# A transformer block on one core: stored results of one query block loaded ahead of the attention's end, two weight loads moved, five casts moved to GpSimd

## The chip, the cores and the metric

The kernel runs on one core of one Trainium2 chip. The metric is the device time of one execution in microseconds (us). The engines are TensorE (PE, with PEld for its weight loads), VectorE (DVE), ScalarE (ACT), GpSimd (POOL) and SyncE (SP), which here only issues DMA transfers.

## The reference

One block of a transformer with conditioned layer norms, for 2048 tokens of width 448, all in float32:

```python
mod = (_silu(c) @ w_mod).reshape(c.shape[0], 6, 1, -1)
sa, ca, ga, sb, cb, gb = (mod[:, i] for i in range(6))
h = _layernorm(x) * (1 + ca) + sa
x = x + ga * attention(h, wqkv, wo)          # 16 heads of 28, full softmax, then @ wo
h = _layernorm(x) * (1 + cb) + sb
y = _layernorm(h)
x = x + gb * (gelu(y @ w1 + b1) @ w2 + b2)   # 448 -> 1792 -> 448
```

## The kernel before

Products in full precision are made of three: an operand is split into a high part, rounded to TensorE's faster float32 form (a cast), and a low part, the rest (a subtraction), and high by high, high by low and low by high are summed. So each weight and each activation needs a cast and a subtraction before it is used.

The attention goes through 16 units. A unit is one of 4 groups of four heads and one of 4 blocks of 512 queries (blocks 0 to 3), group by group; so units 12 to 15 are the last group's blocks 0 to 3. A unit has 16 steps, one for each 128 keys: TensorE makes scores (`s`), ScalarE takes their exponentials (`slot_c`, `slot_c0h`, `slot_d` and others), TensorE sums them with the values (`o`). Beside this TensorE computes the scores once more in the other layout (`m`, and `s` in a pair) for the units to come, and VectorE takes their row maxima (`mxp`). Side work hangs on step numbers: `at(step, fn)` puts `fn` on a list, and behind the matmuls of each step the loop runs what is listed for it. Each engine takes its instructions in the order in which this Python code issues them; nothing reorders them. SP's queue is one such order: an issue that waits holds up all behind it.

A unit's output is scaled by its softmax sums (tasks `t_den`, `t_rec`, `t_split`, `t_split2`, some steps into the next unit), split into high and low, and stored: groups 0 to 2 in `dpk` (named `o` in the trace), and unit 14, the last group's block 2, in `down` (named `w`). `project` then multiplies 128 tokens of a block by the output weights `wo` and adds to `acc`. It wants four things of the block: the high rows, the low rows, the mixed rows (the third group's rest, both parts, in four pieces), all loaded by `load_o`, and the last group's own part. For blocks 0 and 1 this happens within the attention; block 2 (`NB - 2`) is projected in the MLP's first iterations, and block 3 later.

The output weights are prepared at steps 178 to 188 (`wo_item`): GpSimd multiplies the raw weights by `ga`, the first product is cast for the high part (`wo_p[0]`, `slot_e` in the trace), and GpSimd subtracts for the low part (`wo_p[1]`).

Behind the attention comes the MLP: for each block, 14 iterations of a first product (`mlp1`, 11 matmuls, gelu on ScalarE, split) and, two iterations later, a second product (`mlp2`, 12 matmuls). W1 and W2 are prepared by `w_prep`, a list of items in order of use: W1's first quarter (items 0 to 3), W2's first quarter (4 to 7), W1's second (8 to 11), and so on. An item's raw tile (one of three, `raw`) is loaded by SP two items ahead, then VectorE casts and subtracts, in W2's case after a multiplication by `gb` into `full`. Ten items are done in the last unit's steps, the others in the MLP's iterations.

The second layer norm of block 0 runs in the last unit too: its tokens are transposed on VectorE in two halves (`turn` and `slot_a2h`), stored to `y_dr`, and loaded again. Two steps of this matter here: `turn` is written and stored at steps 242 and 243, and the tiles `d0h` and `d0i`, which belong to the maxima of pairs in the first units, are free later until W2's third quarter takes them.

The last unit starts at step 240 (`last0`). What the changed lines do before:

```python
    load_o(NB - 2, 2, "c1")     # behind the last step, ahead of mlp1(0, 0)
    load_o(NB - 2, 3, "c0h")
...
    at(last0 + 2, lambda: w_prep.load(2))
```

Of the kernel before, what the change touches and what calls it, by code (L numbers as in the profile page):

```python
# [13 lines left out]
F32 = mybir.dt.float32  # L14
F32R = mybir.dt.float32r
# [7 lines left out]
D = 448  # L23
# [4 lines left out]
NB = S // 512  # L28
NG = H // 4
NKT = S // 128  # L30
# [19 lines left out]
def tile_adaln_block(ctx: ExitStack, tc: tile.TileContext, x, x_t, wqkv, wo, w1, b1, w2, b2, c, w_mod, out):  # L50
    nc = tc.nc
    pe, act, dve, pool, sp = nc.tensor, nc.scalar, nc.vector, nc.gpsimd, nc.sync
# [27 lines left out]
    def nm(t):  # L80
        uid[0] += 1
        return f"{t}_{uid[0]}"

    def sbt(tag, shape, dt=F32, bufs=1):
        return sb.tile(shape, dt, tag=tag, name=nm(tag), bufs=bufs)

    def slot(tag, shape, dt=F32R):
        return sb.tile(shape, dt, tag="slot_" + tag, name=nm("slot_" + tag), bufs=1)
# [24 lines left out]
    def ps_mx():  # L113
        mx_ring.append(mx_ring.pop(0))
        return ps_tile(mx_ring[-1], 1 if mx_ring[-1] == "m1" else 2)
# [7 lines left out]
    def f(t):  # L123
        return t.bitcast(F32)
# [313 lines left out]
    def put_ones(g):  # L438
        sp.dma_start(f(dscr[1][0][g])[DH:128:32, :], ones_d)
# [22 lines left out]
    def mm_acc(p, terms):  # L462
        for i, (a, b) in enumerate(terms):
            pe.matmul(p, a, b, start=(i == 0), stop=(i == len(terms) - 1))  # L464
# [438 lines left out]
    for n, i in (  # L903
# [7 lines left out]
        p, ts = firsts[n]  # L911
# [4 lines left out]
    for b in range(NB):  # L916
# [11 lines left out]
        for n, (tb, kind, g) in enumerate(tasks):  # L928
# [28 lines left out]
            if more:  # L957
                k = n - (6, 4, 4, 4)[b]
# [66 lines left out]
    wo_p = [slot(f"e{part}", [128, NG, D]) for part in range(2)]  # L1025
# [22 lines left out]
    def wo_item(n):  # L1048
        def ld(r):
            if n == 4:  # L1050
                pool.memset(r[:, :D], 0.0)
                for j in range(4):
                    sp.dma_start(r[32 * j : 32 * j + DH, :D], wo[NP + DH * j : NP + DH * j + DH, :])
                return
            p0 = 0
            for r0, r1 in (((128 * n, 128 * n + 128),), MIX_HI, MIX_LO)[max(0, n - 1)]:
                sp.dma_start(r[p0 : p0 + r1 - r0, :D], wo[r0:r1, :])
                p0 += r1 - r0

        def go(r):  # L1060
            full = sbt("full", [128, 512], bufs=3)
            ps = slice(0, 112 if n == 3 else 128)
            pool.tensor_tensor(out=full[ps, :D], in0=r[ps, :D], in1=rows["ga"][ps], op=ALU.mult)

            def rest():
                if n == 3:
                    hi = sbt("hi", [128, 512], F32R, bufs=3)
                    dve.tensor_copy(hi[ps, :D], full[ps, :D])
                    pool.tensor_tensor(out=wo_p[1][ps, 2, :], in0=full[ps, :D], in1=f(hi)[ps, :D], op=ALU.subtract)
                    pool.tensor_copy(wo_p[1][0:32, 2, :], f(hi)[0:32, :D])  # L1070
                    return
                k = min(n, 3)
                dve.tensor_copy(wo_p[0][:, k, :], full[:, :D])
                if n != 2:
                    pool.tensor_tensor(out=wo_p[1][:, k, :], in0=full[:, :D], in1=f(wo_p[0])[:, k, :], op=ALU.subtract)

            at(WO_AT + 2 + 2 * n, rest)

        return ld, go
# [5 lines left out]
    down = [dr.tile([128, 512], F32R, tag=f"w{part}", name=f"w{part}", bufs=1) for part in range(2)]  # L1085
    o_in = {}

    def load_o(qt, n, tag):
        t = slot(tag, [128, 2, 512])
        o_in[(qt, n)] = t  # L1090
        cs = slice(qt * 512, (qt + 1) * 512)
        if n < 2:
            sp.dma_start(f(t), f(dpk[n])[0:256, cs].rearrange("(k p) n -> p k n", p=128))
        elif n == 2:
            for k, pieces in enumerate((zip((0, 1), MIX_HI), zip((1, 0), MIX_LO))):
                p0 = 0
                for part, (r0, r1) in pieces:
                    sp.dma_start(f(t)[p0 : p0 + r1 - r0, k, :], f(dpk[part])[r0:r1, cs])
                    p0 += r1 - r0
        else:  # L1100
            for part in range(2):
                sp.dma_start(f(t)[:, part, :], f(down[part]))

    def wo_terms(qt, own):
        hi, lo, mix = (o_in[(qt, n)] for n in range(3))
        w_hi, w_lo = wo_p
        terms = []
        for k in range(2):
            terms += [(hi[:, k], w_hi[:, k, :]), (hi[:, k], w_lo[:, k, :]), (lo[:, k], w_hi[:, k, :])]
        terms += [(mix[:, 0], w_hi[:, 2, :]), (mix[0:112, 1], w_lo[0:112, 2, :])]  # L1110
        o_hi, o_lo = own
        return terms + [(o_hi, w_hi[:, 3, :]), (o_hi, w_lo[:, 3, :]), (o_lo, w_hi[:, 3, :])]

    def project(qt, t, own):
        p = ps_mx()
        ts = slice(t * 128, (t + 1) * 128)
        mm_acc(p[:, :D], [(x[:, ts], w) for x, w in wo_terms(qt, own)])
        if qt >= NB - 2:
            dve.tensor_tensor(out=acc[qt][:, t, :], in0=p[:, :D], in1=acc[qt][:, t, :], op=ALU.add)
            return  # L1120
        y = sbt("full", [128, 512], bufs=3)[:, :D]
        act.copy(y, p[:, :D])
        pool.tensor_tensor(out=acc[qt][:, t, :], in0=acc[qt][:, t, :], in1=y, op=ALU.add)
# [67 lines left out]
    def ln2_stages(b):  # L1191
# [27 lines left out]
        halves = {}  # L1219

        def turn(t):
            if b:
                if t == 0:
                    turned.append(slot("e1", [128, 14, 4, 32], F32))
                to = turned[0][:, :, t, :]
            else:
                if t == 0:
                    turned.append(None)
                if t % 2 == 0:
                    halves[t // 2] = slot("a2h", [128, 14, 2, 32], F32) if t else sbt("turn", [128, 14, 2, 32])  # L1230
                to = halves[t // 2][:, :, t % 2, :]
            dve.transpose(to, ys[t][:, :D].rearrange("p (c j) -> p c j", j=32))

# [25 lines left out]
        for t in range(4):  # L1259
            own = 20 if 0 < b < NB - 1 else 0  # L1260
            at_stage = (
                (t, 4 + t, 6 + t, 10 + t // 2, 10 + t),
                (t, 4 + t, min(6 + t, 8), 9, 30 + t),
                (t // 2, 2 + t // 2, 4 + t // 2, 6 + t // 2, own + 10 + t),
            )[min(b, 2)]
            for i, fn in zip(at_stage, (lambda t=t: stat(0, t), lambda t=t: mid(t), lambda t=t: stat(1, t), lambda t=t: fin(t), lambda t=t: addb(t))):
                plan.setdefault(i, []).append(fn)
            plan.setdefault(11 + t // 2 if not b else 10 if b < 2 else 7 + t // 2, []).append(lambda t=t: turn(t))
# [79 lines left out]
    NU = NG * NB  # L1348
    sched = {}

    def at(step, fn):
        sched.setdefault(step, []).append(fn)

    wo_prep = Prep([wo_item(n) for n in range(5)])
    for i in range(2 * NC):
        h, k = divmod(i, NC)
# [21 lines left out]
    for qt in range(NB - 2):  # L1378
        for n, tag in enumerate(("a2h", "a3h", "b1h")):
            at(NKT * (NU - NB + qt + 1) - 3, lambda qt=qt, n=n, tag=tag: load_o(qt, n, tag))  # L1380
    for n, tag in enumerate(("a3h", "b1h")):
        at(NKT * (NU - 1), lambda n=n, tag=tag: load_o(NB - 2, n, tag))
    for i in range(5):
        at(1 + i, lambda: put_spare(1))
    for g in (1, 2):
        at(6 + g, lambda g=g: put_ones(g))
    at(WO_AT + 11, b2_load)
    at(WO_AT + 24, b2_mul)
    last0 = NKT * (NU - 1)
# [12 lines left out]
    items += [w1_item(3, k, ("c1", "c1h")) for k in range(NC)]  # L1402
    items += [w2_item(ft, ("e0",)) for ft in range(12, NFT)]
    w_prep = Prep(items)
    at(last0 + 2, lambda: w_prep.load(2))
    for k in range(10):
        at(last0 + 5 + k + (k >= 4), w_prep.step)

# [46 lines left out]
    for u in range(NU):  # L1455
        g, qt = divmod(u, NB)
# [71 lines left out]
    def mlp1(b, i, mid=None):  # L1528
        q, ii = divmod(i, 4)
        w_hi, w_lo = w1t[q]  # L1530
        fs = slice(ii * 128, (ii + 1) * 128)
        p = ps_mx()
        ts = terms448(*yT[b], lambda k: w_hi(k)[:, fs], lambda k: w_lo(k)[:, fs])
        mm_acc(p, [(w, y) for y, w in ts])
        if mid:
            mid()
        gf = sbt("full", [128, 512], bufs=3)
        if (b, i) == (0, 0):
            act.activation(gf[:, 0:1], zero_col, AF.Gelu_apprx_tanh)
        act.activation(gf, p, AF.Gelu_apprx_tanh, bias=b1_col[:, i : i + 1])  # L1540
        ghi = sbt("hi", [128, 512], F32R, bufs=3)
        glo = sbt("lo", [128, 512], F32R, bufs=3)
        (dve.tensor_copy if b else act.copy)(ghi, gf)  # L1543
        dve.tensor_tensor(out=glo, in0=gf, in1=f(ghi), op=ALU.subtract)  # L1544
        gs[(b, i)] = (ghi, glo)

    load_o(NB - 2, 2, "c1")
    load_o(NB - 2, 3, "c0h")
    mlp1(0, 0)
    av(*pend)  # L1550
    end_unit(pend[0], pend[3])
    tail = {}
    assert len(sched) == 8
    for t in range(4):
        tail[1 + t] = [lambda t=t: project(NB - 2, t, [o_in[(NB - 2, 3)][:, part] for part in range(2)])]
    tail[1].append(lambda: load_o(NB - 1, 1, "c1h"))
    tail[4] += [lambda: load_o(NB - 1, 0, "c1"), lambda: load_o(NB - 1, 2, "b1h")]
    for n, k in zip((0, 0, 4, 5, 6, 7, 8, 8), sorted(sched)):
# [91 lines left out]
```

## Time and profile before

| | |
|---|---|
| median of 3 runs | 1086.80 us (1086.71 to 1086.81) |
| the profiled execution's own time | 1086.78 us |
| its span | 1085.0 us |
| mean granted TensorE clock | 0.997 of full speed |
| busy share of the span | PE 99%, PEld 60%, DVE 74%, ACT 64%, POOL 24% |

The profile is one execution of the program, its times counted from the start of the span. A row of the timeline has the start, the time that the rows merged in it take, the engine, the line of the code (`L464` is the helper in which most products are issued, so there the names tell more), the operation, what it writes and reads, and in square brackets how long the engine had been idle before it, and what ended that. `SPq` rows are DMA issues on SyncE's queue. The page's row of the granted clock, in tenths for 40 equal slices of the span, drops from 9 in one slice alone:

```profile
PE   8999999999999999999999999999989999999998
PEclk9999999999999999999999999999989999999999
```

The place of that 8 is the slice from 787 to 814 us (30th of 40 slices of 27.1 us), just behind the last unit.

### The profile page before, as it was taken

The numbers are of one execution on the slowest core, as the hardware profiler recorded it, in microseconds if no ns is written. First come the engines' busy times: TensorE is split into PE (matmuls) and PEld (weight loads), VectorE is DVE, ScalarE is ACT, GpSimd is POOL, SyncE is SP. The second block draws the span as 40 slices with busy tenths as digits, with TensorE's granted clock in tenths as the row PEclk, the third lists the DMA queues.
The fourth block names the chain that finished last, engine by engine and source line by source line (L and its number), as shares of the span: only waits on it lengthen the run. The fifth ranks groups of instructions, "written<-read, shape, count | busy, mean of one in ns | idle before, by whom it ended". The sixth has DMA issues, their size and how long they took to land. (4 is left out here: it accounts for less than half of the span.)

```text
span 1085.0 us, 20661 instructions
## 1 busy us (share of the span) xinstructions
PE 1070.8 (99%) x8175; PEld 652.1 (60%) x8175; DVE 797.9 (74%) x1361; ACT 693.8 (64%) x874; POOL 264.2 (24%) x240
## 2 busy tenths in 40 slices
PE   8999999999999999999999999999989999999998
PEld 6766764444444444444444444554478888888887
DVE  6977878999999989888888887675555565464322
ACT  4567768888888888888888888778833321211111
POOL 1586620011001101034512410126414032061000
PEclk9999999999999999999999999999989999999999
DMA  9444370111231111343434330113543301002000
GB/s 312 174 172 146 122 233 21 61 53 52 63 103 59 50 48 28 96 122 83 126 94 120 112 105 31 58 31 94 151 130 96 105 35 43 31 34 73 34 1 34
DMA packets 70335, 95.99 MB, mean 88 GB/s; under 512 B 22331, under 2 KB 34894, under 8 KB 70226
## 3 DMA queue, kind: packets, MB, share of 16 engines
q1 hardware_dynamic: 69754, 93.93, 28.2%
q8 instruction: 64, 1.05, 0.4%
q10 hardware_dynamic: 148, 0.46, 0.1%
q0 software_dynamic: 336, 0.28, 0.1%
q14 instruction: 33, 0.27, 0.1%
HBM read 64.73 MB, written 31.57 MB: 89 GB/s over the span
## 5 line engine op out<-in xcount | busy, mean ns | idle before, releaser
L550 DVE TENSOR_REDUCE mxp<-m 128x1 f32<-128x512 f32 x554 | 358.9, 686 | 69.9 <-PE m L545 58.4
L1492 PE MATMUL s<-slot_b,slot_a 28*128 28x512 f32 (+1 forms) x3072 | 356.6, 425 | 0.1
L1492 PEld LDWEIGHTS s<-slot_b,slot_a 28*128 28x128 f32 (+1 forms) x3072 | 210.5, 183 | 181.3 <-ACT slot_c L1505 99.9
L545 PE MATMUL m<-kh,qh 28*128 28x512 f32 x593 | 217.2, 473 | 0.0
L1505 ACT ACTIVATE slot_c<-s 128x1024 f32<-128x1024 f32 x170 | 174.7, 1027 | 51.1 <-PE s L1492 50.3
L1447 PE MATMUL o<-slot_c,v 128*32 128x512 f32 x680 | 178.9, 605 | 0.0
L1540 ACT ACTIVATE full<-m,b_col 128x512 f32<-128x512 f32 x56 | 38.5, 688 | 196.0 <-PE m L464 187.5
L759 DVE TENSOR_REDUCE mxp<-s 128x2 f32<-128x1024 f32 x117 | 143.4, 1226 | 6.0 <-PE s L545 0.8
L1447 PE MATMUL o<-slot_c1h,v 128*32 128x512 f32 x512 | 134.7, 605 | 0.0
L1447 PE MATMUL o<-slot_c0h,v 128*32 128x512 f32 x508 | 133.6, 605 | 0.0
L1505 ACT ACTIVATE slot_c1h<-s 128x1024 f32<-128x1024 f32 x128 | 130.8, 1022 | 0.0
L1505 ACT ACTIVATE slot_c0h<-s 128x1024 f32<-128x1024 f32 x127 | 130.5, 1028 | 0.0
L1505 ACT ACTIVATE slot_d<-s 128x1024 f32<-128x1024 f32 x86 | 88.3, 1026 | 26.1 <-PE s L1492 25.5
L1543 DVE CAST hi<-full 128x512 fp32r<-128x512 f32 x42 | 19.0, 453 | 102.8 <-ACT full L1540 102.7
L545 PEld LDWEIGHTS m<-kh,qh 28*128 28x128 f32 x593 | 86.2, 181 | 12.7 <-DVE mxp L550 10.9
L1447 PE MATMUL o<-slot_d,v 128*32 128x512 f32 x344 | 90.5, 605 | 0.4 <-ACT osb L1411 0.4
L1148 POOL TENSOR_TENSOR osb<-osb,osb 128x512 f32<-128x512 f32 x16 | 20.5, 1281 | 283.1 <-DMA osb<-drec 262.3
L1544 DVE TENSOR_TENSOR lo<-full,hi 128x512 fp32r<-128x512 f32 x56 | 46.1, 824 | 27.6 <-ACT hi L1543 22.2
L464 PE MATMUL m<-y,slot_a 128*128 128x512 f32 x160 | 60.3, 393 | 0.1
L545 PE MATMUL s<-kh,qh 28*128 28x512 f32 x234 | 52.0, 439 | 0.0
L1447 PEld LDWEIGHTS o<-slot_c,v 128*32 128x32 f32 x680 | 24.5, 108 | 38.4 <-issue 36.6
L723 DVE CUSTOM_DVE_ANT_0 slot_d0i<-m,slot_d0i 128x512 f32<-128x512 f32 x51 | 35.3, 692 | 14.6 <-PE m L545 12.1
(370 smaller groups left out, 1845.4 us busy)
## 6 DMA issues: line engine op xcount, KB each, us to landing
slot_b<-d SPq DMA_DIRECT2D x32, 256.0 KB
slot_a<-d SPq DMA_DIRECT2D x32, 256.0 KB
d<-lo SPq DMA_DIRECT2D x28, 256.0 KB
d<-hi SPq DMA_DIRECT2D x16, 256.0 KB
osb<-drec SPq DMA_DIRECT2D x15, 256.0 KB
out_dram<-xn SPq DMA_DIRECT2D x16, 224.0 KB
raw<-in_B_w_dram SPq DMA_DIRECT2D x14, 224.0 KB
qh<-d SPq DMA_DIRECT2D x12, 256.0 KB
```

Source lines behind the costliest of these rows:

```text
L464: pe.matmul(p, a, b, start=(i == 0), stop=(i == len(terms) - 1))
L545: pe.matmul(m, qh_sb[(g, qt)][js, i * 128 : (i + 1) * 128], k[js, :], start=True, stop=True)
L550: dve.tensor_reduce(out=mxp[(g, qt)][:, i, j, cch : cch + 1], in_=m, op=ALU.max, axis=AX.X)
L723: dve.tensor_tensor_reduce(out=r, in0=p, in1=r, scale=1.0, scalar=-3.0e38, op0=ALU.add, op1=ALU.max, accum_out=mxp[(g, qt)][:, i, j, cch + ...
L759: dve.tensor_reduce(out=mxp[(g, qt)][:, i, j : j + 2, cch], in_=t, op=ALU.max, axis=AX.X)
L1148: pool.tensor_tensor(out=st["on"], in0=o_sb, in1=st["rb"], op=ALU.mult)
L1447: pe.matmul(o[32 * j : 32 * j + 32, :], v_sb[kt // 4][:, kt % 4, 4 * g + j, :], p[j // 2][:, j % 2, :], start=(kt == 0), stop=(kt == NKT - 1),
L1492: pe.matmul(s2[:, jj, :], ks[rows_, kp, kc], qs[rows_, qp, :], start=(term == 0), stop=(term == 2))
L1505: act.activation(pt[hf], s2, AF.Exp, scale=SCALE)
L1540: act.activation(gf, p, AF.Gelu_apprx_tanh, bias=b1_col[:, i : i + 1])
L1543: (dve.tensor_copy if b else act.copy)(ghi, gf)
L1544: dve.tensor_tensor(out=glo, in0=gf, in1=f(ghi), op=ALU.subtract)
```

## The change

It has three parts. The loads of block 2's mixed rows and of its own part move from behind the last step to steps 248 and 253, into other tiles: the mixed rows into `turn`, which gets the size of two rows of 512, and the own part into `d0h` and `d0i`. W1's first two raw loads move from step 242 to step 234. And the five casts of `wo_item` move from VectorE to GpSimd.

```diff
             def rest():
                 if n == 3:
                     hi = sbt("hi", [128, 512], F32R, bufs=3)
-                    dve.tensor_copy(hi[ps, :D], full[ps, :D])
+                    pool.tensor_copy(hi[ps, :D], full[ps, :D])
...
                 k = min(n, 3)
-                dve.tensor_copy(wo_p[0][:, k, :], full[:, :D])
+                pool.tensor_copy(wo_p[0][:, k, :], full[:, :D])
...
+    def load_own(qt):
+        o_in[(qt, 3)] = [slot(tag, [128, 1, 512])[:, 0, :] for tag in ("d0h", "d0i")]
+        for part in range(2):
+            sp.dma_start(f(o_in[(qt, 3)][part]), f(down[part]))
+
     def load_o(qt, n, tag):
-        t = slot(tag, [128, 2, 512])
+        t = slot(tag, [128, 2, 512]) if tag != "turn" else sbt(tag, [128, 2, 512], F32R)
...
-                    halves[t // 2] = slot("a2h", [128, 14, 2, 32], F32) if t else sbt("turn", [128, 14, 2, 32])
+                    halves[t // 2] = slot("a2h", [128, 14, 2, 32], F32) if t else sbt("turn", [128, 2, 512]).rearrange(
+                        "p a n -> p (a n)"
+                    )[:, : 2 * D].rearrange("p (c t j) -> p c t j", t=2, j=32)
...
+    at(NKT * (NU - 1) + 8, lambda: load_o(NB - 2, 2, "turn"))
+    at(NKT * (NU - 1) + 13, lambda: load_own(NB - 2))
...
-    at(last0 + 2, lambda: w_prep.load(2))
+    at(last0 - 6, lambda: w_prep.load(2))
...
-    load_o(NB - 2, 2, "c1")
-    load_o(NB - 2, 3, "c0h")
...
-        tail[1 + t] = [lambda t=t: project(NB - 2, t, [o_in[(NB - 2, 3)][:, part] for part in range(2)])]
+        tail[1 + t] = [lambda t=t: project(NB - 2, t, o_in[(NB - 2, 3)])]
```

SP's queue before, from the last load of W1's second quarter (two halves) through block 2's mixed rows (`slot_c`, four pieces out of the stored `o`) and its own part (`slot_c0h`, out of the stored `w`) to the next W2 load:

```order
L1311 DMA raw_10922<-in_B_w_dram 64x512
L1312 DMA raw_10922<-in_B_w_dram 64x512
L1098 DMA slot_c_2554_10925<-o_2011 80x512
L1098 DMA slot_c_2554_10925<-o_2012 48x512
L1098 DMA slot_c_2554_10925<-o_2012 32x512
L1098 DMA slot_c_2554_10925<-o_2011 80x512
L1102 DMA slot_c0h_10930<-w_2013 128x512
L1102 DMA slot_c0h_10930<-w_2014 128x512
L1330 DMA raw_10971<-in_B_w_dram 128x448
```

SP's queue now, from the first load of W2's first quarter to the last of W1's second: the mixed rows go into `turn`, the own part into `slot_d0h` and `slot_d0i`, behind the stores `w` of its two parts.

```order
L1334 DMA raw_10683<-in_B_w_dram 128x448
L1103 DMA turn_10707<-o_2011 80x512
L1103 DMA turn_10707<-o_2012 48x512
L1103 DMA turn_10707<-o_2012 32x512
L1103 DMA turn_10707<-o_2011 80x512
L1334 DMA raw_10714<-in_B_w_dram 128x448
L1334 DMA raw_10777<-in_B_w_dram 128x448
L1334 DMA raw_10808<-in_B_w_dram 128x448
L1167 DMA w_2013<-hi_10810 128x512
L1167 DMA w_2014<-lo_10811 128x512
L1313 DMA raw_10844<-in_B_w_dram 128x512
L1091 DMA slot_d0h_10868<-w_2013 128x512
```

The four mixed-row loads moved up past seven weight loads (eight issues) and the two stores, and the own part past three weight loads (four issues): the second own load, then the weight loads of 128x512, follow the last row shown.

GpSimd's order before, from the second multiplication of the raw output weights (`full`) to the first cast of the unit's output (`osb` into `hi`):

```order
L1063 TENSOR_TENSOR full_8396<-raw_8190,row_b2g_8221 128x448
L1075 TENSOR_TENSOR slot_e_488_2010<-full_8330,slot_e_487_2009 128x448
L1063 TENSOR_TENSOR full_8466<-raw_8332,row_b2g_8221 128x448
L1051 MEMSET raw_8468 128x448
L1075 TENSOR_TENSOR slot_e_488_2010<-full_8396,slot_e_487_2009 128x448
L1063 TENSOR_TENSOR full_8537<-raw_8398,row_b2g_8221 112x448
L1063 TENSOR_TENSOR full_8598<-raw_8468,row_b2g_8221 128x448
L1148 TENSOR_TENSOR osb_8404<-osb_8258,osb_8404 128x512
L1069 TENSOR_TENSOR slot_e_488_2010<-full_8537,hi_8601 112x448
L1070 CAST slot_e_488_2010<-hi_8601 32x448
L1158 CAST hi_8639<-osb_8404 128x512
```

GpSimd's order now, from the same multiplication to the cast of the fourth piece:

```order
L1063 TENSOR_TENSOR full_8396<-raw_8190,row_b2g_8221 128x448
L1073 CAST slot_e_487_2009<-full_8330 128x448
L1075 TENSOR_TENSOR slot_e_488_2010<-full_8330,slot_e_487_2009 128x448
L1063 TENSOR_TENSOR full_8466<-raw_8332,row_b2g_8221 128x448
L1051 MEMSET raw_8468 128x448
L1073 CAST slot_e_487_2009<-full_8396 128x448
L1075 TENSOR_TENSOR slot_e_488_2010<-full_8396,slot_e_487_2009 128x448
L1063 TENSOR_TENSOR full_8537<-raw_8398,row_b2g_8221 112x448
L1073 CAST slot_e_487_2009<-full_8466 128x448
L1063 TENSOR_TENSOR full_8598<-raw_8468,row_b2g_8221 128x448
L1150 TENSOR_TENSOR osb_8404<-osb_8258,osb_8404 128x512
L1068 CAST hi_8601<-full_8537 112x448
```

Each cast moved from VectorE's order into GpSimd's, ahead of the subtraction that uses it; a fifth follows the rows shown, and nothing else on either engine changed places.

More of the change, by code (lines that the diff above doesn't have):

```diff
@@ L1093, in load_o @@
             sp.dma_start(f(t), f(dpk[n])[0:256, cs].rearrange("(k p) n -> p k n", p=128))
-        elif n == 2:
+        else:
             for k, pieces in enumerate((zip((0, 1), MIX_HI), zip((1, 0), MIX_LO))):
@@ L1099, in load_o @@
                     p0 += r1 - r0
-        else:
-            for part in range(2):
-                sp.dma_start(f(t)[:, part, :], f(down[part]))
     def wo_terms(qt, own):
```

## The prediction, made before the changed kernel was run

> **What bounds the kernel now.** I read the page's busy shares first, then who TensorE waited for, then the stretch of its longest wait by windows, then that stretch instruction by instruction.
>
> ```profile
> PE 1070.8 (99%) x8175; PEld 652.1 (60%) x8175; DVE 797.9 (74%) x1361; ACT 693.8 (64%) x874; POOL 264.2 (24%) x240
> PE m L464 <- DMA slot_c<-o: 5.7, 2, 4.3
> 778.00:785.60 7.60, 7.54 (x36) 4.83 (x34) 7.29 (x12) 3.87 (x6) 2.81 (x3) 1.00 0.46 145
> 790.00:795.50 5.50, 4.03 (x10) 3.05 (x11) 1.49 (x3) 0.00 (x0) 0.71 (x1) 0.50 0.91 289
> ```
>
> TensorE carries the kernel. Behind the attention, from 778 us to the end, its matmuls waited in one place alone: twice for `slot_c<-o`, together 5.7 us. Those are the stored attention results of block 2, wanted by its first projection. The two windows (columns: length, busy time of PE, PEld, DVE, ACT and POOL, granted clock, DMA share, GB/s) lie ahead of the longer wait and behind it: full clock, then 5.5 us at a granted clock of 0.50. So the wait costs more than its own length. Behind it TensorE waits for nothing more, so whatever is saved here reaches the end.
>
> **Term 1: the wait for block 2's results.**
>
> ```profile
> 785.33 0.36 PE L464 MATMUL m<-slot_e,slot_b1h 128*128 128x448 f32 x1
> 789.96 0.71 PE L464 MATMUL m<-slot_e,slot_c 128*128 128x448 f32 x1 [4.27 <-DMA slot_c<-o]
> 792.14 0.71 PE L464 MATMUL m<-slot_e,slot_c 112*128 112x448 f32 x1 [1.47 <-DMA slot_c<-o]
> ...
> 795.48 0.46 PE L464 MATMUL m<-y,slot_b 128*128 128x512 f32 x1
> ...
> 798.17 0.36 PE L464 MATMUL m<-slot_e,slot_b1h 128*128 128x448 f32 x1
> ...
> 799.39 0.37 PE L1584 MATMUL s<-slot_v,hi 128*128 128x448 f32 x1
> ...
> 801.82 0.39 PE L464 MATMUL m<-y,slot_b 128*128 128x512 f32 x1
> ...
> 802.73 0.39 PE L464 MATMUL m<-y,slot_b 128*128 128x512 f32 x1
> ```
>
> From the last matmul ahead of the wait (785.33) to the first one back near full speed (795.48) pass 10.15 us. In them start six matmuls of a projection and four of an MLP's first product. The next projection does the same six in 799.39 - 798.17 = 1.22 us, the next first product the same four in 802.73 - 801.82 = 0.91 us. So 10.15 - 2.13 = 8.0 us are lost, 5.7 to the wait and 2.3 to the slow clock behind it. With all operands there in time the change gets the 8.0 us back. Are they there? Without the wait TensorE wants the mixed rows at 785.5, the own part (high) at 785.9 and (low) at 786.4.
>
> ```profile
> 759.90 5.93 DMA osb<-drec
> 765.86 0.47 SPq L1312 DMA_DIRECT2D raw<-in_B_w_dram  x1
> 767.48 0.33 SPq L1330 DMA_DIRECT2D raw<-in_B_w_dram  x1
> 773.94 1.95 SPq L1330 DMA_DIRECT2D raw<-in_B_w_dram  x2
> 776.04 0.33 SPq L1165 DMA_DIRECT2D w<-hi  x1
> 777.42 0.33 SPq L1165 DMA_DIRECT2D w<-lo  x1
> 778.86 4.55 SPq L1309 DMA_DIRECT2D raw<-in_B_w_dram  x3
> ...
> 786.52 1.93 SPq L1098 DMA_DIRECT2D slot_c<-o  x4
> 788.56 0.83 SPq L1102 DMA_DIRECT2D slot_c0h<-w  x2
> ```
>
> *Mixed rows, four loads.* Before, they are issued at 786.52, behind every weight load of the last steps. Now they stand ahead of the second W2 load (767.48). Their tile was last read by the stores of the first transposed half, long landed by then. They read results stored units earlier. Their issues take 1.93 us, so even one after another by 773.9, where SP next has something to do, they are 11 us ahead of need: no wait is left here.
>
> *Own part, two loads.* They must follow the stores `w<-hi` (776.04) and `w<-lo` (777.42) and now stand behind the weight load of 778.86. Neither a store's landing nor this load is timed in the trace. The bounds:
>
> ```profile
> 752.37 1.91 DMA y_dr<-turn
> 783.08 2.65 DMA raw<-in_B_w_dram
> ```
>
> A store of the same queue took 1.91 us, a 256 KB load 2.65 us in quiet traffic, 5.93 us (`osb<-drec`) at worst. Low store landed at 777.42 + 1.9 = 779.3; low part issued by 779.9 (one issue is 0.3 to 0.4 us), landed at 782.6 with 2.65 us, at 785.8 with 5.93. All of it is ahead of 786.4. If the store also took 5.93 us: 783.4 + 0.4 + 5.9 = 789.7, a wait of 3.3 us. I take the quiet price, because the windows show 145 GB/s there, half of the 289 of the crowded one; the 3.3 us stay for the range.
>
> *What is queued behind.* Behind the own loads on SP wait the raw loads of W1's second quarter. Each needs a raw tile that VectorE gives back, so that three issues of 0.33 us spread over 4.55 us (778.86 to 783.41); SP's wait for the store until 779.3 and two issues lie inside the first gap, so nothing is pushed. At 786.5 SP is now rid of six issues (2.8 us), which is to the good of the loads after it. The two tiles of the own part were last used many steps earlier, and the W2 quarter that takes them next comes after the last projection.
>
> **What would be late next.** TensorE would come 8 us earlier to everything behind 786 us.
>
> ```profile
> 777.80 1.03 DVE L1340 TENSOR_TENSOR full<-raw,row_gb 128x448 f32<-128x448 f32 x1
> 780.97 1.28 ACT L1539 ACT_TABLE_LOAD   x1 [2.37 <-DVE slot_a L1343]
> 786.27 0.68 ACT L1540 ACTIVATE full<-m,b_col 128x512 f32<-128x512 f32 x1
> 786.40 0.69 DVE L1544 TENSOR_TENSOR lo<-full,hi 128x512 fp32r<-128x512 f32 x1
> 794.01 0.63 DVE L1119 TENSOR_TENSOR acc<-m,acc 128x448 f32<-128x448 f32 x1 [4.82 <-PE m L464]
> 808.98 0.39 PE L464 MATMUL m<-y,slot_v 128*128 128x512 f32 x1
> ```
>
> By the matmul rows a first product takes 2.5 us, a projection 2.2, a second product 2.4. So the next first product starts at 786.6, the second projection at 789.1, the first second product at 791.3, the one after at 793.7. Their needs: the bank of the gelu at 786.27, free at 787.0 (2.1 us to spare); the low part made at 786.40, there at 787.1 (4.2 us); the bank of the first projection, added by VectorE, which idles 4.82 us ahead of 794.01 and so does it at 789.2 (3.9 us). The matmul of 808.98, first on W1's second quarter, would start at 801.0; the last piece of that quarter is prepared right behind the add, now about 790.4. The smallest margin is 2.1 us. Term 1 stays 8.0 us.
>
> **Term 2: five casts from VectorE to GpSimd.**
>
> ```profile
> L1073 DVE CAST slot_e<-full x4: 331/383/385, 594.3 to 612.6; 128x448 fp32r<-128x448 f32 x4
> L1158 POOL CAST hi<-osb x13: 604/610/1008, 218.9 to 775.0; 128x512 fp32r<-128x512 f32 x13
> 607.63 1.00 DVE L1068 CAST hi<-full 112x448 fp32r<-112x448 f32 x1
> 607.09 1.29 POOL L1148 TENSOR_TENSOR osb<-osb,osb 128x512 f32<-128x512 f32 x1
> 608.71 1.16 POOL L1069 TENSOR_TENSOR slot_e<-full,hi 112x448 fp32r<-112x448 f32 x1 [0.33 <-DVE mxp L542]
> 608.80 0.69 DVE L550 TENSOR_REDUCE mxp<-m 128x1 f32<-128x512 f32 x1
> 610.68 1.03 ACT L1505 ACTIVATE slot_c<-s 128x1024 f32<-128x1024 f32 x1 [0.35 <-PE s L1492]
> 613.59 1.02 ACT L1505 ACTIVATE slot_d<-s 128x1024 f32<-128x1024 f32 x1 [0.81 <-PE s L1492]
> 618.02 1.02 ACT L1505 ACTIVATE slot_c<-s 128x1024 f32<-128x1024 f32 x1 [0.37 <-PE s L1492]
> ```
>
> Four casts took 0.33 to 0.39 us; I count no loss for them. The fifth began while GpSimd multiplied (607.09 to 608.38) and took 1.00 us; the maxima behind it, and TensorE which waits for them, came late: the next exponential of the same half waited 0.81 us for TensorE, and the step took 613.59 - 610.68 = 2.91 us, against (618.02 - 613.59) / 2 = 2.2 in the two behind it. That is 0.7 us that go with the cast. Between nothing (another wait takes its place) and 0.7 I take 0.7: the steps behind give nothing back. On GpSimd five casts come in, 0.6 us each by its casts of a 128x512 tile (median 610 ns), 3 us in all on an engine 24% busy, which no longer waits for VectorE there; nothing wants the output weights before the projections units later. The cost is nothing.
>
> The Trainium skill ("SBUF — State Buffer", section "SBUF: two separate sides") has a rule that speaks against this: VectorE and GpSimd share a pair of ports under an exclusive lock, held for the whole instruction, so that each added GpSimd cast may stop a VectorE instruction that needs the pair. What that would do here is the second rival below; with it the sum would be 8.7 - 3 = 5.7 us saved.
>
> **Term 3: W1's first two loads eight steps sooner.**
>
> ```profile
> 749.29 0.95 SPq L1309 DMA_DIRECT2D raw<-in_B_w_dram  x2
> 755.20 0.35 DVE L1321 CAST slot_b<-raw 128x512 fp32r<-128x512 f32 x1
> ```
>
> They move ahead of the last unit's maxima and the loads of block 2's first rows. Two issues, 0.95 us: that much could be won or lost on SP. But VectorE takes the first tile at 755.20 without a wait, and the stores behind them on SP go at 752.37, when VectorE has made their data. The third load, which VectorE does wait for, stays where it was. Zero.
>
> **Sum.** 8.0 + 0.7 = 8.7 us. The profiled execution took 1086.78 us around its span of 1085.0 us and stands on the median (1086.80). So 1086.8 - 8.7 = 1078.1 us, a span near 1076.3.
>
> **Rivals.**
> *A shorter wait stays* (0.13): the own part is late. Priced above: up to 3.3 us of wait, 1081.4 us; if the clock also falls as it did behind the 4.27 us, up to 2.3 more, 1083.7. The Trainium skill ("TensorE: Matmul & The Clock Gate", section "What's actually happening") puts the fall behind an idle window of some 3.4 us; by it a shorter wait can cost only itself, and 1081.4 would stand. The trace shows no wait between 1.5 and 4.3 us that could tell.
> *The added casts hold VectorE up* (0.04): VectorE's fifth cast took 1.00 us beside GpSimd in place of 0.38, so the two do get in each other's way. Were each of five casts of 0.6 us to stop a maximum for its whole length, 3.0 us would be lost: 1081.1 us. Against it: the maximum of 608.80 took its 0.69 us beside GpSimd's 1.16 us, and VectorE does little but maxima there. So far the trace bears the lock out for casts only.
> *The wait only changes its name* (0.05): an eviction or a weight becomes the bound as TensorE comes early. Against it stand the margins of 2.1 us and more; it would have to take 6.5 of the 8.7 us to end within 0.2%, at 1084.6 or above.
> *Slower* (0.03): the four mixed-row issues push the W2 load behind them. SP issues only when an earlier transfer has landed: the issue at 765.86 came the moment `osb<-drec` had (759.90 + 5.93). So that load could go at 773.9 in place of 767.48 and land by 779.8 in place of VectorE's 777.80; the gelu's table load follows VectorE's work on that tile (780.97), and TensorE waits once this is over 2.1 us late. It decides from 2.1 + 8.7 = 10.8 us of delay on, which no transfer of this trace comes near: with 14 us, 1090.0.
> *More is saved* (0.03): freed VectorE time speeds up other steps; 1077 or a little below.
>
> **Numbers.** The forecast has 0.72, its own range 1077.4 to 1079.2 (with no gain from the casts and a wait of some tenths). The range for 8 in 10 reaches below into the last rival and above through the first two: 1076.8 to 1082. A measurement tells about 0.2%, 2.2 us: faster (below 1084.6) has 0.72 + 0.13 + 0.04 + 0.03 = 0.92, same 0.05, slower 0.03.
>
> **What would show it.** Right: TensorE's first projection runs through, the granted clock stays at 1.0 from 785 to 800, VectorE no longer idles 4.8 us, the loads `turn<-o` go out near 767 to 774 and the own loads near 779 to 780; the step at 610 us takes 2.3. Wrong: a wait of TensorE for `slot_d0h` or `slot_d0i`, or for `hi`, `lo` or a weight between 786 and 802.

## The result, and the profile after

| | before | after |
|---|---|---|
| median | 1086.80 us (1086.71 to 1088.67, 4 runs) | 1078.61 us (1077.36 to 1079.04, 4 runs) |
| the profiled execution | 1086.78 us, span 1085.0 | 1077.36 us, span 1075.6 |
| predicted | | 1078.1 us (1076.8 to 1082.0) |

The ratio is 0.9919, with a 95% interval of 0.9901 to 0.9936: 8.2 us faster by the medians. The profiled execution of after is the fastest of its four; its difference to before, 9.4 us, is what the traces below add up to.

The page of after: the busy times and the granted clock in 40 slices.

```profile
PE 1067.0 (99%) x8175; PEld 650.1 (60%) x8175; DVE 796.1 (74%) x1356; ACT 693.6 (64%) x874; POOL 266.7 (25%) x245
PEclk9999999999999999999999999999999999999999
```

The 8 in the clock's 30th slice is gone. TensorE's waits from 700 us to the end, in us, times and the longest, now hold a single row, from the attention; the 5.7 us for `slot_c<-o` have no successor:

```profile
PE o L1453 <- ACT osb L1417: 0.4, 1, 0.4
```

The windows around the block's end (length, busy time of PE, PEld, DVE, ACT and POOL, granted clock, DMA share, GB/s), and TensorE's timeline there, from the last matmul that both kernels share to the fifth of the next first product:

```profile
784.00:788.00 4.00, 4.00 (x20) 3.45 (x19) 3.93 (x9) 2.45 (x4) 0.73 (x2) 1.00 0.68 189
788.00:792.00 4.00, 4.00 (x22) 3.69 (x21) 3.33 (x8) 1.77 (x3) 0.71 (x1) 1.00 0.74 243
```

```profile
783.97 0.36 PE L464 MATMUL m<-slot_e,slot_b1h 128*128 128x448 f32 x1
784.17 0.58 PE L464 MATMUL m<-slot_e,turn 128*128 128x448 f32 x2
784.59 0.57 PE L464 MATMUL m<-slot_e,slot_d0h 128*128 128x448 f32 x2
785.00 0.36 PE L464 MATMUL m<-slot_e,slot_d0i 128*128 128x448 f32 x1
...
786.13 0.39 PE L464 MATMUL m<-y,slot_b 128*128 128x512 f32 x1
```

From `slot_b1h` to the fifth matmul of the first product pass 786.13 - 783.97 = 2.16 us, where before 10.15 us passed: 8.0 us saved, at full clock throughout. At `slot_b1h` this run was already 785.33 - 783.97 = 1.36 us ahead: 0.5 us were there at 580 us, ahead of the first instruction that the change moves (0.2 of them since 16 us, behind loads of the start), 0.6 us came in the steps of the casts (below), and 0.2 us in small pieces behind them. 1.4 + 8.0 = 9.4.

SP's queue in after, with the loads in their new place:

```profile
765.97 3.64 SPq L1103 DMA_DIRECT2D turn<-o  x4
769.71 4.78 SPq L1334 DMA_DIRECT2D raw<-in_B_w_dram  x3
774.63 0.34 SPq L1167 DMA_DIRECT2D w<-hi  x1
776.02 0.33 SPq L1167 DMA_DIRECT2D w<-lo  x1
777.46 0.33 SPq L1313 DMA_DIRECT2D raw<-in_B_w_dram  x1
777.88 0.38 SPq L1091 DMA_DIRECT2D slot_d0h<-w  x1
778.36 0.38 SPq L1091 DMA_DIRECT2D slot_d0i<-w  x1
```

The own part goes out 6.7 and 6.6 us before TensorE takes it at 784.59 and 785.00. The four mixed-row issues take 3.64 us instead of 1.93: by SP's row of waits 1.6 us of it are three waits for earlier loads (`xn<-y_dr`, 1.0 us the longest), and one of the issues itself took 1.28 us, where the four of before took 0.41 to 0.53 each.

### The profile page after: what moved, and what is told of

It reads as the page before. It is cut to its first block, busy times and chain, and to the rows that moved or that the text cites. A ratio compares the mean times of both kernels' runs of the same rounds, so it can differ in the third digit from the quotient of the medians.

```text
span 1075.6 us, 20660 instructions
## 1 busy us (share of the span) xinstructions
PE 1067.0 (99%) x8175; PEld 650.1 (60%) x8175; DVE 796.1 (74%) x1356; ACT 693.6 (64%) x874; POOL 266.7 (25%) x245
## 3 DMA queue, kind: packets, MB, share of 16 engines
q8 instruction: 64, 1.05, 0.4%
## 4 chain that ended last, share of the span: by engine, by line
PE 97%; DVE 1%; DMA 1%; ACT 1%; issue 0%; SPq 0%; ACTq 0%; DVEq 0%
PE s L1498 24%; PE o L1453 24%; PE m L464 17%; PE pa L464 9%; PE m L545 6%; PE s L1588 3%; PE s L1590 3%; PE s L1589 3%; PE s L545 2%; PE ma L545 2%; PE t L1590 1%; PE t L1588 1%; PE t L1589 1%; DMA slot_c<-in_w_mod_dram 1%; PE o L342 0%
```

## The experiments

Three questions were open: which part carries the 8 us, why the clock falls behind a wait, and what the casts are worth. Each group of kernels below is compared with before on the same chip: 1087.05 us there for the three parts alone and the doubled casts, 1087.12 for the late loads, 16 extra matmuls and the one moved cast, 1087.11 for the rest.

### Each part alone

**The loads alone**, on before:

```diff
+    at(NKT * (NU - 1) + 8, lambda: load_o(NB - 2, 2, "turn"))
+    at(NKT * (NU - 1) + 13, lambda: load_own(NB - 2))
...
-    load_o(NB - 2, 2, "c1")
-    load_o(NB - 2, 3, "c0h")
```

> The kernel before with the block-2 loads moved alone (mixed rows into turn at step 248, own part into d0h and d0i at step 253); casts and W1's first loads stay. Theory (the loads carry the gain, 8.0 us of it: 5.7 us of wait and 2.3 us of slow clock): 8.0 us faster than before, 1078.8 us, TensorE without a wait in the first projection, granted clock 1.0 there. Rival (the earlier W1 loads are needed to keep SP's queue and the W2 loads in time): a wait of TensorE or a W2 load that lands late remains, 1080 to 1083 us.

1078.23 us (1077.97 to 1078.92), ratio 0.9919 (0.9904 to 0.9934). TensorE waits no more than in after, and the clock holds:

```profile
788.00:792.00 4.00, 4.00 (x22) 3.65 (x21) 3.37 (x7) 2.21 (x4) 0.71 (x1) 1.00 0.72 236
```

The moved loads carry all of the gain that can be measured, and they need neither of the other parts.

**The casts alone**, on before:

```diff
-                    dve.tensor_copy(hi[ps, :D], full[ps, :D])
+                    pool.tensor_copy(hi[ps, :D], full[ps, :D])
...
-                dve.tensor_copy(wo_p[0][:, k, :], full[:, :D])
+                pool.tensor_copy(wo_p[0][:, k, :], full[:, :D])
```

> The kernel before with the five casts moved to GpSimd alone. Theory: 0.6 us faster than before, 1086.2 us; in the trace the step whose exponential started at 610.68 takes 2.3 us in place of 2.91, and the wait for block 2's results stays at 5.7 us. Rival (shared ports: GpSimd's casts hold VectorE's maxima up): up to 3 us slower, 1089.8 us, with maxima longer than 0.69 and 1.23 us beside the casts.

1086.21 us, ratio 0.9993 (0.9984 to 1.0003). The long step at 610 us is 2.30 us long, as expected; the 0.8 us between the medians is less than the interval resolves.

**W1's loads alone**, on before:

```diff
-    at(last0 + 2, lambda: w_prep.load(2))
+    at(last0 - 6, lambda: w_prep.load(2))
```

> The kernel before with W1's first two loads at step 234 alone. Theory: no change, 1086.8 us; VectorE takes the two tiles at the same distance from the end of the last step as before. Rival (they free SP and the transfers around 750 us): the third and fourth W1 loads land sooner and up to 0.9 us is gained, 1085.9 us.

1086.70 us, ratio 0.9997 (0.9988 to 1.0006): no change. VectorE's waits for the third and fourth load, in before first and in this kernel second (timeline; in brackets the idle time and what ended it):

```profile
766.30 0.43 DVE L1321 CAST slot_b<-raw 128x512 fp32r<-128x512 f32 x1 [8.89 <-DMA raw<-in_B_w_dram]
771.45 1.46 DVE L1321 CAST slot_b<-raw 128x512 fp32r<-128x512 f32 x1 [3.99 <-DMA raw<-in_B_w_dram]
```

```profile
765.23 0.43 DVE L1321 CAST slot_b<-raw 128x512 fp32r<-128x512 f32 x1 [8.62 <-DMA raw<-in_B_w_dram]
770.38 0.51 DVE L1321 CAST slot_b<-raw 128x512 fp32r<-128x512 f32 x1 [3.99 <-DMA raw<-in_B_w_dram]
```

The first two loads were not late, and the two that were are issued where they always were.

### Each of the two loads left late

**The own part behind the last step**, all else as in after:

```diff
-    at(NKT * (NU - 1) + 13, lambda: load_own(NB - 2))
...
+    load_own(NB - 2)
     mlp1(0, 0)
```

> The changed kernel with the loads of the own part left behind the last step (into d0h and d0i as now), the mixed rows at step 248. SP then issues them behind the last weight load of W1's second quarter, in the changed kernel's time at about 785.1 and 785.5; with 2.65 us they land near 788. TensorE wants them at 784.6 and 785.0. Theory: a wait of about 3 us and nothing else, 1081.7 us; if the clock falls as it did behind the wait of 4.27 us, up to 2.3 us more, 1084.0 us. Rival (the loads were ready in time from there too, so that only the mixed rows mattered): 1078.6 us.

1083.91 us (1082.47 to 1084.20, 7 runs), ratio 0.9968 (0.9957 to 0.9979): 5.3 us of the gain gone. SP's issue and TensorE's wait, and the window:

```profile
785.05 0.58 SPq L1091 DMA_DIRECT2D slot_d0h<-w  x1
...
788.13 1.12 PE L464 MATMUL m<-slot_e,slot_d0h 128*128 128x448 f32 x2 [3.41 <-DMA slot_d0h<-w]
789.49 0.74 PE L464 MATMUL m<-slot_e,slot_d0i 128*128 128x448 f32 x1 [0.24 <-DMA slot_d0i<-w]
```

```profile
788.00:792.00 4.00, 3.63 (x8) 2.58 (x9) 1.73 (x3) 0.29 (x1) 0.57 (x1) 0.50 0.72 263
```

A wait of 3.41 us took the clock down as the 4.27 us of before had. From the start of the last `slot_b1h` matmul ahead of the wait to the start of the next projection this trace takes 794.27 - 783.94 = 10.33 us, and after takes 787.71 - 783.97 = 3.74. So 6.6 us are lost here in the traces: 3.65 to the two waits and 2.9 to the slow clock.

**The mixed rows behind the last step**, all else as in after:

```diff
-    at(NKT * (NU - 1) + 8, lambda: load_o(NB - 2, 2, "turn"))
...
+    load_o(NB - 2, 2, "turn")
     mlp1(0, 0)
```

> The changed kernel with the loads of the mixed rows left behind the last step (into turn as now), the own part at step 253. SP issues the four loads at about 785.1 to 787.0; landing takes up to 4 us as before, so the second mixed product starts near 790.5 in place of 784.4. Theory: a wait of some 6 us and the slow clock behind it (2.3 us), so nearly all of the gain is lost: 1085.5 to 1086.9 us. Rival (it was the own part that held the projection): 1078.6 to 1080 us.

1085.86 us (10 runs), ratio 0.9989 (0.9980 to 0.9999): nearly all of the gain gone.

```profile
788.37 0.71 PE L464 MATMUL m<-slot_e,turn 128*128 128x448 f32 x1 [4.29 <-DMA turn<-o]
789.51 0.71 PE L464 MATMUL m<-slot_e,turn 112*128 112x448 f32 x1 [0.42 <-DMA turn<-o]
```

Here too the granted clock is 0.50 from 788 to 792 us. So the loads must both move. With either of the two left late, less than half of the gain is there: the projection needs both, and TensorE waits for whichever comes last.

### Why the clock falls

Two explanations stood against each other: TensorE standing still, or the crowded DMA queues of that stretch (289 GB/s before). In before, extra matmuls whose result is overwritten fill a part of the wait (16 of them, the cut shown), or the whole (32):

```diff
+        if (qt, t) == (NB - 2, 0):
+            for _ in range(16):
+                pe.matmul(p[:, :D], o_in[(qt, 0)][:, 0, ts], wo_p[0][:, 0, :], start=True, stop=True)
```

**16 extra matmuls.**

> The kernel before, its loads where they were, with 16 additional matmuls of 448 columns (0.2 us each, 3.2 us) ahead of block 2's first projection, written to the bank that the projection then starts afresh. They fill part of the wait. Theory (2.3 of the 8.0 us came from the clock, which falls when TensorE stands still for 4.3 us): the transfer ends when it did, the wait ahead of the first mixed product shrinks to about 1.0 us, the clock stays at 1.0 and the time falls by about 2 us to 1084.5 us, though TensorE does more work. Rival (the slow matmuls behind the wait come from the transfers' traffic, 289 GB/s, and not from standing still): they stay slow, 1086.8 us.

1086.69 us (10 runs), ratio 0.9996 (0.9986 to 1.0005): not faster, so the expectation missed.

```profile
783.43 3.40 PE L1119 MATMUL m<-slot_e,slot_a3h 128*128 128x448 f32 x16
...
788.68 0.44 PE L464 MATMUL m<-slot_e,slot_c 128*128 128x448 f32 x1 [0.63 <-DMA slot_c<-o]
790.89 0.44 PE L464 MATMUL m<-slot_e,slot_c 112*128 112x448 f32 x1 [1.77 <-DMA slot_c<-o]
```

```profile
792.00:796.00 4.00, 4.00 (x12) 3.19 (x12) 2.63 (x5) 0.56 (x1) 0.00 (x0) 0.57 0.78 270
```

The waits shrank by 3.3 us, as much as the filler takes. But two short waits, 0.63 and 1.77 us, with one matmul between them, brought the slow clock too, and with some delay: the matmuls at 788.68 and 790.89 still ran in 0.44 us, and then it fell, to 0.57 from 792 to 796. That is the profiled execution. Seven of the ten have its mean granted clock of 0.998 and a median of 1087.32 us; three have 1.000 and a median of 1086.15. So the fall may be missing in some executions, of which no trace was kept, but even those are not near the 1084.5 us expected.

**32 extra matmuls.**

> The kernel before with 32 additional matmuls (6.5 us) ahead of block 2's first projection in place of the 16 of the run before, so that TensorE is busy until the transfers land (second mixed product at 790.9 there). Theory (the clock falls because TensorE stands still, also in pieces: 0.63 and 1.77 us with one matmul between were enough): no wait, granted clock 1.0 through 796 us, and though TensorE does 6.5 us more of work, the time falls by the 2.3 us of the clock, to about 1084.7 us. Rival (the clock falls with the transfers' traffic): the matmuls behind 791 us stay slow, 1086.7 us or more.

1084.69 us (10 runs), ratio 0.9979 (0.9969 to 0.9989): 6.5 us of useless work added, and 2.4 us saved.

```profile
783.67 6.65 PE L1119 MATMUL m<-slot_e,slot_a3h 128*128 128x448 f32 x32
...
791.38 0.57 PE L464 MATMUL m<-slot_e,slot_c 128*128 128x448 f32 x2
```

```profile
792.00:796.00 4.00, 4.00 (x20) 3.36 (x19) 2.77 (x5) 1.36 (x3) 0.00 (x0) 1.00 0.83 282
```

No wait for the loads is left and the clock stays at 1.00, beside 282 GB/s. Standing still is the cause, not the traffic. From the start of the first projection, with its filler, to the start of the second this trace takes 794.93 - 783.67 = 11.26 us, before's 797.16 - 784.32 = 12.84: 1.6 of the 2.4 us are shown at this place, the rest lies within the interval (1.2 to 3.4 us).

**The old loads kept beside the new ones**, into two tiles that nothing reads, in after:

```diff
+    o2, o3 = o_in[(NB - 2, 2)], o_in[(NB - 2, 3)]
+    load_o(NB - 2, 2, "c1")
+    idle = slot("c0h", [128, 2, 512])
+    for part in range(2):
+        sp.dma_start(f(idle)[:, part, :], f(down[part]))
+    o_in[(NB - 2, 2)], o_in[(NB - 2, 3)] = o2, o3
     mlp1(0, 0)
```

> The changed kernel with the old loads kept beside the new ones: the mixed rows and the own part are loaded a second time behind the last step, into c1 and c0h, and nobody reads these copies. So the traffic of the kernel before is there at its old time, 6 issues (2.8 us) stand on SP's queue again, but TensorE has its operands. Theory: no wait, clock 1.0, as the changed kernel within 0.3 us, 1078.6 us. Rival (traffic lowers the clock, or SP's queue carried a part of the gain): 1080 to 1082 us.

1078.30 us (1076.99 to 1078.52), ratio 0.9915 (0.9898 to 0.9931), the same as after.

```profile
792.00:796.00 4.00, 4.00 (x20) 3.47 (x19) 2.21 (x5) 1.78 (x3) 0.00 (x0) 1.00 0.95 314
```

The clock holds at 314 GB/s, which settles the traffic from the other side. The six issues that SP was rid of behind the last step (2.8 us) carried nothing of the gain that the times resolve. The same trace has one wait that left the clock alone, at the end of the attention: 0.88 us ahead of 779.69, with a granted clock of 1.00 from 776 to 788 us.

```profile
779.69 0.50 PE L464 MATMUL m<-y,slot_a 128*128 128x512 f32 x1 [0.88 <-POOL y L1297]
```

```profile
776.00:784.00 8.00, 7.12 (x39) 4.27 (x32) 7.69 (x12) 4.75 (x7) 3.70 (x4) 1.00 0.69 217
```

**The own part late, with 8 extra matmuls**, to make the wait about 1.8 us:

```diff
-    at(NKT * (NU - 1) + 13, lambda: load_own(NB - 2))
...
+    load_own(NB - 2)
     mlp1(0, 0)
...
+        if (qt, t) == (NB - 2, 0):
+            for _ in range(8):
+                pe.matmul(p[:, :D], o_in[(qt, 0)][:, 0, ts], wo_p[0][:, 0, :], start=True, stop=True)
```

> The kernel with the own part loaded behind the last step, and 8 additional matmuls (1.6 us) ahead of the projection: the one wait shrinks from 3.4 to 1.8 us. Theory A (a wait this short keeps the clock): 1083.9 less some 2 us, 1081.8 us. Theory B (any wait of this kind brings the slow clock, if TensorE's work in the window falls low enough): the clock falls still, 1083.9 us.

1082.37 us, ratio 0.9955 (0.9937 to 0.9972). The four runs with their mean granted clock:

```
1083.19 us at 0.998 (profiled)   1081.36 us at 0.999
1083.50 us at 0.998              1081.54 us at 1.000
```

```profile
788.47 0.68 PE L464 MATMUL m<-slot_e,slot_d0h 128*128 128x448 f32 x2 [1.90 <-DMA slot_d0h<-w]
...
790.23 0.63 PE L464 MATMUL m<-y,slot_a 128*128 128x512 f32 x1
```

In the profiled run one wait of 1.90 us was followed, 1.8 us after it had ended, by matmuls of 0.63 us instead of 0.39. The two runs with the higher mean clock were 1.9 us shorter, which fits a fall that comes in one execution and not in the next; no trace shows one of the shorter two, so that reading is not shown. Theory A's 1081.8 us lies near these two and theory B's 1083.9 near the others, so neither is settled.

### What the casts are worth

**Each of the five casts issued twice on GpSimd**, in after:

```diff
-                    pool.tensor_copy(hi[ps, :D], full[ps, :D])
+                    for _ in range(2):
+                        pool.tensor_copy(hi[ps, :D], full[ps, :D])
...
-                pool.tensor_copy(wo_p[0][:, k, :], full[:, :D])
+                for _ in range(2):
+                    pool.tensor_copy(wo_p[0][:, k, :], full[:, :D])
```

> The changed kernel with each of the five casts issued twice on GpSimd (the same result written twice). Theory (GpSimd has the room and VectorE's maxima are not held up): as the changed kernel, 1078.6 us, within a few tenths. Rival (each GpSimd cast stops a VectorE instruction for its length): 5 x 0.57 = 2.9 us more, 1081.5 us.

1077.63 us (1077.23 to 1077.93), ratio 0.9912 (0.9897 to 0.9927): ten casts cost no more than five.

```profile
607.40 0.69 DVE L550 TENSOR_REDUCE mxp<-m 128x1 f32<-128x512 f32 x1 [0.17 <-PE m L545]
607.65 1.19 POOL L1069 CAST hi<-full 112x448 fp32r<-112x448 f32 x2
```

The maximum beside the doubled cast keeps its 0.69 us, and so does every one from 590 to 616 us; the longer maxima (over `s`) all keep their 1.23 us.

**Only the fifth cast moved**, on before, one execution:

```diff
-                    dve.tensor_copy(hi[ps, :D], full[ps, :D])
+                    pool.tensor_copy(hi[ps, :D], full[ps, :D])
```

> The kernel before with the fifth cast (112 x 448, into hi) alone moved to GpSimd, the other four on VectorE. Theory: the step at 610 us takes 2.3 us in place of 2.91, as with all five moved, so the whole 0.6 us hang on this one cast. Rival (all five shorten steps a little): the step stays above 2.5 us.

1085.68 us, one execution, which decides nothing by itself. The trace decides: the step at 610 us takes 2.28 us, as the theory said. The steps around the casts, from the exponential of `slot_d` near 606 us to that near 620, can be laid side by side over all traces. In before and after they are, first and last:

```profile
606.24 1.02 ACT L1505 ACTIVATE slot_d<-s 128x1024 f32<-128x1024 f32 x1 [0.35 <-PE s L1492]
...
620.30 1.02 ACT L1505 ACTIVATE slot_d<-s 128x1024 f32<-128x1024 f32 x1 [0.33 <-PE s L1492]
```

```profile
605.73 1.02 ACT L1511 ACTIVATE slot_d<-s 128x1024 f32<-128x1024 f32 x1 [0.34 <-PE s L1498]
...
610.16 1.03 ACT L1511 ACTIVATE slot_c<-s 128x1024 f32<-128x1024 f32 x1 [0.34 <-PE s L1498]
...
612.46 1.03 ACT L1511 ACTIVATE slot_d<-s 128x1024 f32<-128x1024 f32 x1 [0.36 <-PE s L1498]
...
619.18 1.02 ACT L1511 ACTIVATE slot_d<-s 128x1024 f32<-128x1024 f32 x1 [0.34 <-PE s L1498]
```

In the table the step at 610 us is the time from the exponential of `slot_c` near 610 us to that of `slot_d` behind it (in after the two rows in the middle). The fifth cast is the prediction's (`hi`, L1068); the last in time is the fourth of L1073.

| kernel | casts on | the stretch | fifth cast | step at 610 us | last cast |
|---|---|---|---|---|---|
| before | VectorE | 14.06 us | 1.00 us | 2.91 us | 0.38 us |
| loads alone | VectorE | 13.90 | 0.83 | 2.75 | 0.38 |
| W1's loads alone | VectorE | 13.79 | 0.54 | 2.46 | 1.05 |
| 32 extra matmuls | VectorE | 13.79 | 0.53 | 2.45 | 1.03 |
| 16 extra matmuls | VectorE | 13.63 | 0.38 | 2.30 | 0.98 |
| fifth cast moved | both | 13.45 | 0.56, GpSimd | 2.28 | 0.81 |
| after | GpSimd | 13.45 | 0.57, GpSimd | 2.30 | 0.57, GpSimd |

In each of the five kernels with the fifth cast on VectorE the step is 1.91 or 1.92 us longer than the cast: what the cast is held, the step is late. With the casts on GpSimd the stretch takes 13.42 to 13.45 us, in all seven such kernels (and in the one with only the fifth moved). On VectorE it takes 0.2 to 0.6 us more, and how much is not set by the code: the same casts take 0.38 us in one kernel and 1.0 us in another. What sets their length is a GpSimd instruction that began before them. First the kernel with the loads alone, then the one with 16 extra matmuls:

```profile
606.32 1.28 POOL L1150 TENSOR_TENSOR osb<-osb,osb 128x512 f32<-128x512 f32 x1
607.02 0.83 DVE L1068 CAST hi<-full 112x448 fp32r<-112x448 f32 x1
```

```profile
607.00 1.53 POOL L1151 TENSOR_TENSOR osb<-osb,osb 128x512 f32<-128x512 f32 x1
607.00 0.38 DVE L1068 CAST hi<-full 112x448 fp32r<-112x448 f32 x1
...
610.89 1.29 POOL L1162 TENSOR_TENSOR lo<-osb,hi 128x512 fp32r<-128x512 f32 x1
611.45 0.98 DVE L1073 CAST slot_e<-full 128x448 fp32r<-128x448 f32 x1
```

In the first pair GpSimd ends at 607.60 and the cast at 607.85. In the last pair it is 612.18 and 612.43; in before 608.38 and 608.63. Three times the cast ends 0.25 us behind GpSimd's instruction, whenever it began, and five more held casts, in the traces of W1's loads alone, of 32 extra matmuls and of the one moved cast, end 0.24 to 0.26 us behind it. In the middle pair the cast began no later than GpSimd and took its 0.38 us, and GpSimd's instruction took 1.53 us in place of 1.28.

## Why the prediction was right, step by step

*Term 1, 8.0 us.* It held to the digit in the traces: 10.15 us became 2.16. Its two pieces, 5.7 us of waiting and 2.3 us of slow clock, were taken apart by the runs. With enough filler (32 matmuls) both go; with half of it (16) the wait shrinks by 3.3 us, but in the profiled execution the clock's part stays. That the sum came within 0.5 us of the median is partly luck: after's four runs lie from 1077.36 to 1079.04, and a sum of 8.0 without term 2 would have fallen as near.

*The mixed rows.* In time, as said. Their issues were priced at 1.93 us and took 3.64; the cover, up to 773.9 us, held that easily. The second W2 load, behind them, went at 769.71 instead of 767.48, and VectorE still multiplied its tile at 776.40, 1.4 us before the 777.80 of before, which is the lead of this run. The rival that made the kernel slower from there did not come near.

*The own part.* The bounds were a landing after 2.65 or 5.93 us. With the own loads left late, TensorE started on them 788.13 - 785.05 = 3.1 and 789.49 - 785.67 = 3.8 us after their issue, in traffic of 181 to 263 GB/s: a little above the quiet price and inside the bounds. The store was priced at 1.9 us; in the kernel with both loads the low part went out at 779.36 behind a store issued at 777.33, 2.0 us later. The 6.6 us between issue and use made both errors free.

*What is late next.* The smallest margin was put at 2.1 us, the gelu's read of the bank that the second projection writes:

```profile
785.29 0.68 ACT L1546 ACTIVATE full<-m,b_col 128x512 f32<-128x512 f32 x1
787.71 0.57 PE L464 MATMUL m<-slot_e,slot_a3h 128*128 128x448 f32 x2
```

It is 787.71 - 785.97 = 1.7 us. Nothing else took the wait's place: VectorE's add, which idled 4.82 us before, now runs at 787.71 without a wait.

*Term 2, 0.7 us: mis-sized.* Its mechanism was right, for the step is late by what the cast is held. It failed where it took one execution's cast of 1.00 us for a cost of the code, and the four other casts, short in that trace, for free: in three other traces the last of them, held in the same way, took 0.98 to 1.05. The fifth was 0.6 us long beyond its own 0.38 because it happened to begin in the middle of a GpSimd instruction; in the other kernels with the casts on VectorE the loss was 0.2 to 0.45 us. In before's profiled run the gain was 14.06 - 13.45 = 0.6 us, near the 0.7 written, but over runs the term is 0.2 to 0.6, and no timed comparison resolves it: the casts alone give a ratio of 0.9993 with 1 inside the interval, and after, which has them moved, is not faster than the loads alone.

*Term 3, zero.* Right, and for the reason given: ratio 0.9997 (0.9988 to 1.0006), the late loads unchanged.

*The rival of a shorter wait* was priced at 1081.4 us for a wait of 3.3 us, and at 1083.7 if the clock fell as well. The own part left late made a wait of that length, 3.41 us (by a late issue, where the rival had a late store), and its time was 1083.91: the dearer of the two. The Trainium skill ("TensorE: Matmul & The Clock Gate", section "What's actually happening") puts the fall behind an idle window of about 3.4 us, from which the prediction drew that a shorter wait might cost only itself. The runs don't bear that out: 0.63 and 1.77 us with a matmul between, and a single wait of 1.90 us, brought the slow clock as well. The same section says that the window runs freely and is not reset when a kernel starts; the two pairs of times around the 1.90 us wait would fit that, but no trace here shows the window.

*The rival of the casts that hold VectorE up* is refuted where it put its price, at the maxima: they keep 0.69 us beside ten casts. The rule behind it was the lock of the Trainium skill ("SBUF — State Buffer", section "SBUF: two separate sides"): the one that starts first holds the pair of ports for its whole instruction. As VectorE's side of the lock the section names instructions in a two-port mode or with two SBUF inputs. The maxima have a single input, a bank that TensorE wrote, so the rival asked more of the rule than it says. Between casts on VectorE and GpSimd's multiplications and subtractions the traces agree with it, in both directions (a cast that ends 0.25 us behind GpSimd's instruction; a GpSimd instruction that takes 1.53 us in place of 1.28). So the rule speaks for the change here, not against it: it is VectorE's casts, not its maxima, that were held.

## What to carry to other kernels

Where the profile shows TensorE waiting for a load, look at the granted clock in the windows behind that wait and price both: here 5.7 us of waiting cost 8.0, and 3.65 us (3.41 and 0.24) cost 5.3 by the medians and 6.6 in the trace. A wait that is only shortened may keep the clock's part of its price, so bring the operands in time altogether, all of them. And before a long instruction in one trace becomes a term of a sum, look which instruction of another engine began just before it; its length may belong to that run alone.

## What the runs showed of the hardware that was not expected

The clock fell after waits far shorter than expected: 2.4 us in two pieces, and 1.90 us in one piece. There it fell only 0.5 us and 1.8 us after TensorE had begun to work again, while behind the waits of 3.41 and 4.27 us the first matmul was already slow; and then it stayed at half for 3 us and more. So matmuls added in front of the wait can make a kernel faster: 32 of them cost 6.5 us of work and took 2.4 us off the whole.

What exactly decides the fall, the length of the wait or its place in time, stays open. One wait of 1.90 us has a fall in its trace, one of 0.88 us has none, and several executions without a trace look like ones in which the clock held, for their mean granted clock was 0.999 or 1.000: two of four with the wait of 1.90 us, three of ten with 16 extra matmuls, and one of seven with the own part late (1082.47 us, the shortest of them).

A cast on VectorE that began while GpSimd multiplied or subtracted and was held by it ended 0.24 to 0.26 us behind GpSimd's instruction, in eight pairs, while VectorE's maxima beside ten GpSimd casts kept their 0.69 and 1.23 us.
